# Later heads' probabilities turned by VectorE in 32x32 blocks and placed by a DRAM write and four reads, in place of TensorE's transposes

## The chip, the cores and the metric

The kernel runs on one core of a Trainium2 chip. The metric is the device time of one execution in microseconds (us). The kernel before takes 1205.58 us, the median of three runs that lie between 1205.02 and 1205.92 us. The engines are named as in the profile: PE is TensorE, DVE is VectorE, ACT is ScalarE, POOL is GpSimd, and SP is SyncE, which here only issues DMAs.

## What is computed

Eight batches of eight attention heads with a decay, 576 tokens and a head width of 64, and behind them a feed-forward block with a layer norm.

```python
scores = q @ k.T / 8 + (cum[:, None] - cum[None, :])     # causal, per head
attn   = softmax(scores)
x      = concat_heads(attn @ v)                          # (8, 576, 512)
xn     = (x - mean(x)) / sqrt(var(x) + 1e-6) * g_ln
out    = x + relu(xn @ w_ch1) @ w_ch2                    # w_ch1: 512 x 2048, w_ch2: 2048 x 512
```

To multiply the probabilities with `v` on PE, the key index has to lie on the partitions, while the softmax has the query index there. The 576 x 576 probabilities of a head must therefore be turned.

## The kernel before

The order of the work is written out by hand. The 64 heads are cut into four row units each, `t` = 1 to 4 (unit 1 takes the first 64 rows, `t` = 0, along); unit `t` has 128 query rows and 192, 320, 448 or 576 keys. One loop runs over the 256 units, and each turn of it is a **slot**. A slot emits the pieces that a string of letters in `ORDERS` names, in that order; all engines run their own instructions in the order in which they were emitted, so the string sets what stands ahead of what on each engine. In the third string, which holds from slot 66 on: `Q` scores of this unit (PE), `S` mask and row minimum (DVE), `A` product with `v` of an older unit (PE), `e` exponential (ACT), `t` and `h` and `l` the turning of an older unit (PE, ACT, DVE), `B` the division by the row sum (DVE makes the reciprocal, POOL multiplies), `M` the first feed-forward product of one step (PE, 12 matmuls of 256 columns), `N` the second one of the step before (PE, 6 matmuls of 512 columns), `r` and `m` the ReLU and its low part (ACT, DVE), `P` and `D` preparations and loads.

The feed-forward work is 18 chunks of 256 tokens by 16 steps, 288 steps in all. From slot 35 on a slot carries one step, and the steps that are left when the slots are used up follow alone. So PE has, in each slot, one step and the attention matmuls of the unit, in one line.

The first 16 heads ("full") compute in f32. The later 48 split each operand in a high part of the type fp32r and a low part, the rest, and add up two or three cheaper products. Only these 48 are touched in substance. For them a unit goes this way before: `softmax_b` scales the rows `p` on POOL (L428) and copies them by a DMA into a tile `pw` of the type fp32r (L441); two slots after its scores (`LAG` = 2) `transpose_unit` turns 128 x 128 pieces of `pw` on PE into a PSUM bank `tr` (L447, by `tr`); `transposed_hi` rounds them on ACT into the high part `ph` (L505); `transposed_lo` makes the low part `pl`, or the lower half of `ph`, on DVE (L510). Three slots after the scores of unit 2 and of unit 4 `av_unit` multiplies (L544): first the products with the high part (`o<-ph,vv`), then those with the low part (`o<-pl,vv`).

```python
def softmax_b(h, t):                       # L428: POOL
    nc.gpsimd.tensor_scalar(out=pt[:m, :w], in0=pt[:m, :w], scalar1=st[:m, 3:4], ...)
def transposed_lo(h):                      # L510: DVE
    nc.vector.tensor_tensor(out=lo, in0=tp, in1=hi.bitcast(F32), op=ALU.subtract)
```

Of the kernel before, what the change touches and what calls it, by code (L numbers as in the profile page):

```python
# [17 lines left out]
P = 128  # L18
# [10 lines left out]
LAG = 2  # L29
FIRST_MOE = 35  # L30
# [21 lines left out]
    (37, "WwQSstAMhPelgNFrfmBDLRba"),  # L52
    (66, "QSAFteahBlMPrmNbRLD"),
# [4 lines left out]
def attn_moe(ctx: ExitStack, tc: tile.TileContext, qk, v, f, g, w1, w2, out):  # L58
# [21 lines left out]
    ident0 = work.tile([P, P], F32, tag="p", bufs=3, name="ident0")  # L80
# [26 lines left out]
    fa = work.tile([B * H, S], F32, tag="p", bufs=3, name="fa")  # L107
    fb = work.tile([B * H, S], F32, tag="p", bufs=3, name="fb")
    fc = work.tile([B * H, S], F32, tag="p", bufs=3, name="fc")
    fones = work.tile([B * H, 704], F32, tag="ph1", bufs=1, name="fones")[:, 0:S]  # L110
# [197 lines left out]
    def load(n):  # L308
        h = Head()
        h.n, h.full = n, n < NFULL  # L310
        if h.full:
            h.kl = work.tile([66, S], F32, tag="kl", bufs=2, name=f"kl{n}")
            if len(xfs) < 2:
                xfs.append(new_xq(f"xf{n}", F32))
            h.xq = xfs[n % 2]
            nc.sync.dma_start(out=h.xq[0:64, :], in_=qk[n][0:64, 0, :])
            nc.sync.dma_start(out=h.kl[0:64, :], in_=qk[n][0:64, 1, :])
            if n > 0:
                nc.sync.dma_start(out=h.kl[64:66, :], in_=cumd[n])
# [15 lines left out]
    def prep_a(h):  # L335
# [47 lines left out]
    corners, padded, words = [], {}, []  # L383
# [39 lines left out]
    def softmax_b(h, t):  # L423
# [7 lines left out]
        if not h.full:  # L431
            if t == 0:
                if not words:
                    words.append(pools["late"].tile([P, D], F32R, tag="pw0", bufs=1, name="pw0"))
                    nc.gpsimd.memset(words[0].bitcast(F32), 0.0)
                pw = words[0]
            elif t % 2 == 0:
                pw = pools["late"].tile([P, S], F32R, tag="pw", bufs=1, name=f"pw{h.n}_{t}")
            else:
                pw = work.tile([P, S], F32R, tag="p", bufs=3, name=f"pw{h.n}_{t}")  # L440
            nc.sync.dma_start(out=pw[:m, :w].bitcast(F32), in_=pt[:m, :w])  # L441
            h.p[t] = (pw, st)
# [12 lines left out]
    def transpose_unit(h, t):  # L455
# [3 lines left out]
        if t <= 2:  # L459
            if t == 1:  # L460
                if h.full:
                    h.ph1 = padded_keys("ph1", 704, S1)
                else:
                    h.ph1 = work.tile([P, 704], F32R, tag="ph1", bufs=1, name=f"ph1_{n}")
                h.pl1 = None if h.full else pools["late"].tile([P, 384], F32R, tag="pl1", bufs=1, name=f"pl1_{n}")
            ph = h.ph1
            pl = ph if h.full else h.pl1
            tp = bank(f"tr{n}_{t}")
            if t == 1:
# [3 lines left out]
                work_.append((tp[0:64, 0:192], ph[0:64, 0:192], ph[64:128, 0:192]))  # L473
                work_.append((tp[:, 192:320], ph[:, 320:448], pl[:, 0:128]))
            else:
# [3 lines left out]
                work_.append((tp[0:64, 0:128], ph[0:64, 192:320], ph[64:128, 192:320]))  # L479
                work_.append((tp[:, 128:384], ph[:, 448:704], pl[:, 128:384]))  # L480
        else:
            if t == 3:
                if h.full:
                    h.ph2 = padded_keys("ph2", 9 * P, S - S1)
                else:
                    h.ph2 = work.tile([P, 9 * P], F32R, tag="ph2", bufs=1, name=f"ph2_{n}")
                h.pl2 = None if h.full else pools["late"].tile([P, 7 * P], F32R, tag="pl2", bufs=1, name=f"pl2_{n}")
            c = 0 if t == 3 else P
            ph = h.ph2[:, : 8 * P].rearrange("p (k c) -> p k c", k=4)[:, :, c : c + P]
            pl = None if h.full else h.pl2[:, : 6 * P].rearrange("p (k c) -> p k c", k=3)[:, :, c : c + P]  # L490
# [3 lines left out]
            work_.append((tp[0:64, 0, :], ph[0:64, 0, :], ph[64:128, 0, :]))  # L494
            work_.append((tp[:, 1:4, :], ph[:, 1:4, :], pl))
            if t == 4:
                tb = bank(f"tr{n}_4b")[:, :P]
                tr(tb, pt[:, 64 + 3 * P : 64 + 4 * P])
                work_.append((tb, h.ph2[:, 8 * P :], None if h.full else h.pl2[:, 6 * P :]))
# [3 lines left out]
    def transposed_hi(h, t):  # L503
        for tp, hi, lo in h.parts:
            nc.scalar.copy(out=hi, in_=tp)  # L505

    def transposed_lo(h):
        if not h.full:
            for tp, hi, lo in h.parts:
                nc.vector.tensor_tensor(out=lo, in0=tp, in1=hi.bitcast(F32), op=ALU.subtract)  # L510

    def av_unit(h, t):
# [25 lines left out]
        vv = h.vv  # L538

        def both(k):  # L540
            return vv[:, k].rearrange("p a d -> p (a d)")

        def acc(o, st, mv, first=False):
            mm(o, st, mv, start=first, stop=True, skip_group_check=True)  # L544

        if t == 2:
            ph, pl, w, c0 = h.ph1, h.pl1, S1, 0
# [3 lines left out]
            acc(po[0:64, 192:320], vv[:, 2, 0, :], pl[:, 256:384])  # L551
            acc(po[0:64, 64:320], vv[:, 1, 0, :], pl[:, 0:256])
        else:
            ph, pl, w, c0 = h.ph2, h.pl2, S - S1, S1
            for k in range(4):
                acc(po[:, 0:256], both(k), ph[:, 256 * k : 256 * k + 256], k == 0)
            acc(po[:, 128:256], both(4), ph[:, 8 * P :])
            acc(po[0:64, 128:256], vv[:, 4, 0, :], pl[:, 6 * P :])
            for k in range(1, 4):
                acc(po[0:64, 0:256], vv[:, k, 0, :], pl[:, 256 * (k - 1) : 256 * k])  # L560
        h.o = (po, w, c0)
# [233 lines left out]
    slots += [None] * (LAG + 1)  # L795
# [15 lines left out]
    for u, slot in enumerate(slots):  # L811
# [8 lines left out]
        if before(LAG + 1) is not None and before(LAG + 1)[1] in (2, 4):  # L820
            av = hd[before(LAG + 1)[0]]
# [7 lines left out]
        def piece(c):  # L829
            tu = before(LAG)  # L830
            if c == "t" and tu is not None:
# [3 lines left out]
            elif c == "l" and tu is not None:  # L835
                transposed_lo(hd[tu[0]])
# [3 lines left out]
            elif c == "A" and av is not None:  # L840
                av_unit(av, before(LAG + 1)[1])
# [18 lines left out]
            elif c == "R":  # L860
                moe.limit = min(NCHUNK, max(0, u - LAG - 1) // (4 * H) * S // C)
# [23 lines left out]
        def next_raw():  # L885
# [14 lines left out]
            elif n == NFULL - 1 and t == 1:  # L900
                load_raw(hd[NFULL], 0)
            elif t in (2, 3) and NFULL < n + 2 < B * H:
                if t == 2:
                    start_head(n + 2)
                load_raw(hd[n + 2], 1 if t == 2 else 0)

        def prep():

            if slot is not None:
                if t == 1 and n + 1 < NFULL:  # L910
                    start_head(n + 1)
                if n + 1 >= NFULL and n + 1 < B * H:
                    if t == 2:
                        prep_a(hd[n + 1])
                    if t == 3:
                        prep_b(hd[n + 1])
                if not h.full and t == LAG + 1:
                    prep_v(h)
                if t == LAG + 1 and h.full and n + 1 < B * H:
                    load_v(hd[n + 1])  # L920
                if t == LAG + 2 and not h.full and n + 1 < B * H:
# [52 lines left out]
```

## Time and profile before

| | |
|---|---|
| median of three runs | 1205.58 us |
| the profiled execution: its time | 1204.13 us |
| the profiled execution: its span, first to last instruction | 1202.3 us |
| DVE busy | 751.5 us (63%) |
| ACT busy | 621.1 us (52%) |
| POOL busy | 457.3 us (38%) |
| moved by DMA | 139.00 MB |

A row of a group gives the line of the kernel, the engine and the operation, what it writes and reads, the shape, the count, and behind the bar the busy time in us and the mean of one in ns. A row of the timeline gives the start in us from the span's start, the duration in us, the engine, line and operation, the shape and how many instructions the row merges; in brackets the idle time of the engine before it and what ended it. A row of the windows gives, for a stretch, the busy time of each engine, then the granted clock of PE as a share of full speed, the mean busy share of the DMA engines and their GB/s. Matmuls overlap: the time from the start of one to the start of the next tells what one occupies, and its duration is longer.

### The profile page before, as it was taken

What the parts mean: (1) busy time and instruction counts of PE and PEld (TensorE: products, weight loads), DVE (VectorE), ACT (ScalarE), POOL (GpSimd) and SP (SyncE); (2) the same over time, 40 slices, a digit from 0 to 9 for tenths busy, and PEclk for the clock granted to TensorE, in tenths of its full rate; (3) what the DMA queues carried; (4) which work ended last, traced back from release to release, by engine and by line L of the source; (5) the groups of instructions that cost most, each with busy time, mean ns of one, the idle gap of its engine ahead of it and who ended that gap; (6) DMA issues with size and microseconds to landing.
All of it is one profiled execution on the core that took longest, in us unless ns stands there. A gap on an engine that the chain in (4) does not pass through costs nothing.

```text
span 1202.3 us, 25770 instructions
## 1 busy us (share of the span) xinstructions
PE 1182.2 (98%) x8368; PEld 1064.2 (89%) x8368; DVE 751.5 (63%) x2658; ACT 621.1 (52%) x1936; POOL 457.3 (38%) x774
## 2 busy tenths in 40 slices
PE   8889999999999999999999999999999999999998
PEld 6567888999999999999999999999999999999997
DVE  6787684576767767777777777767676753122222
ACT  5887575555555555555555555655565532111111
POOL 3445345344545444443545454444454510000000
PEclk9999999999999999999999999999999999999999
DMA  6455442344444343434443434444344321111100
GB/s 194 142 157 170 132 134 84 96 139 132 134 134 134 128 140 125 139 129 145 133 146 123 139 127 132 138 125 143 125 138 132 116 88 40 31 36 40 32 28 26
DMA packets 127541, 139.00 MB, mean 116 GB/s; under 512 B 32432, under 2 KB 100016, under 8 KB 127408
## 3 DMA queue, kind: packets, MB, share of 16 engines
q1 hardware_dynamic: 127408, 137.36, 37.3%
q8 instruction: 67, 1.10, 0.4%
q14 instruction: 66, 0.54, 0.1%
HBM read 79.61 MB, written 19.17 MB: 82 GB/s over the span
## 4 chain that ended last, share of the span: by engine, by line
PE 89%; DVE 4%; ACT 2%; DMA 2%; issue 1%; POOL 0%; SPq 0%; DVEq 0%; ACTq 0%; POOLq 0%
PE h L624 12%; PE h L626 11%; PE h L625 11%; PE acc L646 11%; PE acc L647 11%; PE acc L648 11%; PE o L544 6%; PE tr L447 4%; PE s L378 3%; PE s L377 3%; PE s L375 2%; PE o L519 2%; PE tr L449 1%; DVE p L410 1%; ACT p L421 1%; DMA pw<-p 1%
## 5 line engine op out<-in xcount | busy, mean ns | idle before, releaser
L428 POOL TENSOR_SCALAR p<-p,st 64x64 f32<-64x64 f32 (+4 forms) x320 | 169.6, 535 | 493.3 <-ACT ph L505 173.7
L624 PE MATMUL h<-x,w1h 128*128 128x256 f32 x1152 | 339.2, 294 | 0.4 <-DVE st L410 0.4
L626 PE MATMUL h<-x,w1l 128*128 128x256 f32 x1152 | 325.6, 283 | 0.0
L625 PE MATMUL h<-x,w1h 128*128 128x256 f32 x1152 | 325.4, 282 | 0.0
L421 ACT ACTIVATE p<-p,st 64x64 f32<-64x64 f32 (+4 forms) x320 | 179.1, 560 | 210.2 <-DVE st L410 206.2
L637 DVE SCALAR_TENSOR_TENSOR hh<-h,hh 128x256 fp32r<-128x256 f32 x288 | 120.4, 418 | 186.7 <-ACT hh L632 184.2
L646 PE MATMUL acc<-w2h,hh 128*128 128x512 f32 x576 | 228.1, 396 | 0.0
L647 PE MATMUL acc<-w2l,hh 128*128 128x512 f32 x576 | 227.5, 395 | 0.0
L648 PE MATMUL acc<-w2h,hh 128*128 128x512 f32 x576 | 225.5, 391 | 0.0
L624 PEld LDWEIGHTS h<-x,w1h 128*128 128x128 f32 x1152 | 218.9, 190 | 5.4 <-issue 0.9
L625 PEld LDWEIGHTS h<-x,w1h 128*128 128x128 f32 x1152 | 219.7, 191 | 2.5
L626 PEld LDWEIGHTS h<-x,w1l 128*128 128x128 f32 x1152 | 219.5, 190 | 0.0
L632 ACT ACTIVATE hh<-h 128x256 fp32r<-128x256 f32 x288 | 110.0, 382 | 180.7 <-PE h L626 180.0
L410 DVE CUSTOM_DVE_ANT_0 p<-s,mask 64x64 f32<-64x64 f32 (+4 forms) x320 | 131.0, 423 | 22.5 <-PE s L378 15.0
L648 PEld LDWEIGHTS acc<-w2h,hh 128*128 128x128 f32 x576 | 108.3, 188 | 24.8
L426 DVE TENSOR_SCALAR st<-st 128x1 f32<-128x1 f32 (+1 forms) x320 | 48.1, 150 | 120.7 <-ACT p L421 117.8
L646 PEld LDWEIGHTS acc<-w2h,hh 128*128 128x128 f32 x576 | 109.3, 190 | 14.1 <-ACT ph_full L505 0.2
L647 PEld LDWEIGHTS acc<-w2l,hh 128*128 128x128 f32 x576 | 109.3, 190 | 11.8
L505 ACT CAST ph<-tr 64x128 fp32r<-64x128 f32 (+4 forms) x384 | 107.4, 328 | 3.7 <-PE tr L447 1.4
L580 ACT COPY ot<-o 64x320 f32<-64x320 f32 x96 | 38.0, 396 | 117.4 <-PE o L544 115.4
L510 DVE TENSOR_TENSOR pl<-tr,ph 128x128 fp32r<-128x128 f32 x192 | 88.0, 458 | 4.4
L377 PE MATMUL s<-hi 128*128 128x288 f32 (+4 forms) x288 | 81.8, 297 | 0.0
(90 smaller groups left out, 1884.1 us busy)
## 6 DMA issues: line engine op xcount, KB each, us to landing
raw<-in_qk_dram SPq DMA_DIRECT2D x96, 288.0 KB
wr<-in_w_dram SPq DMA_DIRECT2D x32, 512.0 KB
pw<-p SPq DMA_DIRECT2D x48, 288.0 KB
pw<-p SPq DMA_DIRECT2D x48, 224.0 KB
vr<-in_v_dram SPq DMA_DIRECT2D x64, 160.0 KB
out_dram<-xt SPq DMA_DIRECT2D x36, 256.0 KB
pw<-p SPq DMA_DIRECT2D x48, 160.0 KB
xa<-xs SPq DMA_DIRECT2D x32, 160.0 KB
```

Source lines behind the costliest of these rows:

```text
L377: mm(sp, h.hi[:, 0, q0 : q0 + m], h.hi[:, 1, a:z], start=True, stop=False)
L410: nc.vector.tensor_tensor_reduce(out=pt[:m, a:z], in0=sp, in1=mask[:m, off + a : off + z], scale=-SCALE, scalar=3.0e38 if i == 0 else st[: ...
L421: nc.scalar.activation(pt[:m, :w], pt[:m, :w], AF.Exp, bias=st[:m, i : i + 1], scale=-1.0, accum_out=st[:m, 2:3])
L428: nc.gpsimd.tensor_scalar(out=pt[:m, :w], in0=pt[:m, :w], scalar1=st[:m, 3:4], scalar2=1.0, op0=ALU.mult, op1=ALU.mult)
L624: mm(ph, w1h[:, k, fs], c.x[k][:, 0, :], start=(k == 0), stop=False)
L625: mm(ph, w1h[:, k, fs], c.x[k][:, 1, :], start=False, stop=False)
L626: mm(ph, w1l[:, k, fs], c.x[k][:, 0, :], start=False, stop=(k == KT - 1))
L632: nc.scalar.activation(h[:, 0, :], c.ph, AF.Relu)
L637: nc.vector.scalar_tensor_tensor(out=h[:, 1, :], in0=ph, scalar=0.0, in1=h[:, 0, :].bitcast(F32), op0=ALU.max, op1=ALU.subtract)
L646: mm(c.acc[i], h[:, 0, ts_], w2h[:, j, :], start=(j == 0), stop=False)
L647: mm(c.acc[i], h[:, 0, ts_], w2l[:, j, :], start=False, stop=False)
L648: mm(c.acc[i], h[:, 1, ts_], w2h[:, j, :], start=False, stop=(j == FT - 1))
```

## The change

For the 48 later heads PE no longer turns the probabilities. One slot after its scores (`T`) a unit is turned by DVE, in blocks of 32 x 32, into one tile `pb`; after units 2 and 4 SP writes `pb` to DRAM (`pd`, 128 x 768 or 128 x 1152 elements). Two slots after the scores (`V`, `READ`) four DMAs read it back, one for each 32 partitions, so that each block arrives on its partitions (`pt1`, `pt2`). Four slots after (`HIGH`) ACT makes the high part (`H` and `G`), DVE the low part of the first 64 keys (`l`), and POOL the low part of all others (`o`), in place in `pt`: one instruction of 128 x 896 elements for units 3 and 4, one of 128 x 384 for units 1 and 2. The product follows five slots after (`DONE`) instead of three, and reads `ph` for its high and `pt` for its low products. The columns are now in blocks of 32 with strides, and unit 2's first product takes 384 columns instead of 320. The split of the keys, queries and values moves to other slots (`k`, `x`, `P`), and the copy of the queries from DVE to ACT.

```diff
+READ, HIGH, DONE = 2, 4, 5
...
-    (37, "WwQSstAMhPelgNFrfmBDLRba"),
-    (66, "QSAFteahBlMPrmNbRLD"),
+    (37, "WwkQSTstAMhPeHlgNFGrxfmBoVDLRba"),
+    (66, "kQSTAHeVGFtlahBoMPrxmNbRLD"),
...
-            nc.sync.dma_start(out=pw[:m, :w].bitcast(F32), in_=pt[:m, :w])
-            h.p[t] = (pw, st)
...
+    def turn(h, t):
...
+        nc.vector.transpose(out_[rows, 0:2, first, :], pt[:m, 0:64].rearrange("p (b i) -> p b i", i=32))
+        if t > 0:
+            nc.vector.transpose(
+                out_[:, :, rest : rest + t, :].rearrange("p b k i -> p k b i"),
+                pt[:, 64 : 64 + P * t].rearrange("p (k b i) -> p k b i", b=4, i=32),
+            )
...
+    def write(h, t):
+        w = (6 if t == 2 else 9) * 32
+        pd = dram.tile([P, 4 * w], F32, tag=f"pd{t}", bufs=2, name=f"pd{t}_{h.n}")
+        nc.sync.dma_start(out=pd, in_=turned[0][:, : 4 * w])
...
+    def read(h, t):
...
+        for b in range(4):
+            r = z if b > 1 else 0
+            nc.sync.dma_start(
+                out=pt[32 * b : 32 * b + 32, :].bitcast(F32).rearrange("j (a r) -> j a r", a=4)[:, :, r:],
+                in_=src[b][:, :, r:],
+            )
...
+    def high_first(h, t):
...
+        nc.scalar.copy(out=ph[0:64, :, 0:z, :], in_=pt[0:64, :, 0:z, :].bitcast(F32))
+    def high_rest(h, t):
+        z, pt, ph = parts_of(h, t)
+        nc.scalar.copy(out=ph[:, :, z:, :], in_=pt[:, :, z:, :].bitcast(F32))
+    def low_first(h, t):
+        z, pt, ph = parts_of(h, t)
+        nc.vector.tensor_tensor(
+            out=ph[64:128, :, 0:z, :], in0=pt[0:64, :, 0:z, :].bitcast(F32), in1=ph[0:64, :, 0:z, :].bitcast(F32),
+            op=ALU.subtract,
+        )
+    def low_rest(h, t):
+        z, pt, ph = parts_of(h, t)
+        nc.gpsimd.tensor_tensor(
+            out=pt[:, :, z:, :], in0=pt[:, :, z:, :].bitcast(F32), in1=ph[:, :, z:, :].bitcast(F32), op=ALU.subtract
+        )
...
-            acc(po[:, 0:320], both(0), ph[:, 0:320], True)
-            acc(po[:, 64:320], both(1), ph[:, 320:576])
-            acc(po[:, 192:320], both(2), ph[:, 576:704])
+            acc(0, 384, 0, 0, True)
+            acc(128, 384, 1, 3)
+            acc(256, 384, 2, 5)
```

The names in the rows that follow carry the head and the unit: `p46_4` are the rows of head 46, unit 4, `pt2_45` is what head 45's units 3 and 4 became, `o45_4` their product with `v`.

On POOL, before, these instructions stand between unit 3 and unit 4 of head 46 and behind them:

```order
L428 TENSOR_SCALAR p46_3_10479<-p46_3_10479,st46_3_10480 128x448
L351 TENSOR_TENSOR hi47_10449<-raw47_0_10284,hi47_10449 64x576
L358 TENSOR_TENSOR vv46_10528<-vr46_10323,vv46_10528 128x5x64
L714 TENSOR_TENSOR rs8_10337<-rs8_10337 128x2
L715 TENSOR_TENSOR rs8_10337<-rs8_10337,sv8_10336 128x2
L716 TENSOR_SCALAR rs8_10337<-rs8_10337 128x2
L717 TENSOR_TENSOR rs8_10337<-rs8_10337 128x2
L714 TENSOR_TENSOR rs8_10337<-rs8_10337 128x2
L715 TENSOR_TENSOR rs8_10337<-rs8_10337,sv8_10336 128x2
L428 TENSOR_SCALAR p46_4_10554<-p46_4_10554,st46_4_10555 128x576
```

And now, from unit 4 of head 46 to the place two slots on:

```order
L443 TENSOR_SCALAR p46_4_9980<-p46_4_9980,st46_4_9981 128x576
L513 TENSOR_TENSOR pt2_45_9871<-pt2_45_9871,ph2_45_9986 128x4x224
L783 TENSOR_SCALAR rs8_9781<-rs8_9781 128x2
L784 TENSOR_TENSOR rs8_9781<-rs8_9781 128x2
L345 TENSOR_TENSOR kl48_10031<-raw48_1_9970,hi48_10030 64x576
L443 TENSOR_SCALAR p47_1_10041<-p47_1_10041,st47_1_10042 128x192
L443 TENSOR_SCALAR p0_1_177<-p0_1_177,st47_0_10044 64x64
L365 TENSOR_TENSOR vv46_10085<-vr46_9972,vv46_10085 128x5x64
L443 TENSOR_SCALAR p47_2_10106<-p47_2_10106,st47_2_10107 128x320
L513 TENSOR_TENSOR pt1_46_9989<-pt1_46_9989,ph1_46_10112 128x4x96
L356 TENSOR_TENSOR hi48_10030<-raw48_0_10100,hi48_10030 64x576
```

The two subtractions of L513 are new, and each stands right behind the scaling of another unit's rows in the same slot: the one of head 45's unit 4 behind `p46_4`.

On PE, the next slot opens with the scores of head 47's unit 1, and directly behind them stands the product of head 45's units 3 and 4:

```order
L385 MATMUL s47_0_0_10038<-kl47_9786,xq1_2840 64x128
L606 MATMUL o45_4_10050<-ph2_45_9986,vv45_9840 128x256 x4
L606 MATMUL o45_4_10050<-ph2_45_9986,vv45_9840 128x128
L606 MATMUL o45_4_10050<-pt2_45_9871,vv45_9840 64x256 x3
L606 MATMUL o45_4_10050<-pt2_45_9871,vv45_9840 64x128
```

Before, this place of the slot of unit 1 held the product of units 1 and 2 of the head before and four transposes of its unit 3:

```order
L378 MATMUL s47_0_0_10607<-kl47_10450,xq1_2933 64x128
L544 MATMUL o46_2_10615<-ph1_46_10494,vv46_10528 128x320
L544 MATMUL o46_2_10615<-ph1_46_10494,vv46_10528 128x256
L544 MATMUL o46_2_10615<-ph1_46_10494,vv46_10528 128x128
L544 MATMUL o46_2_10615<-pl1_46_10495,vv46_10528 64x128
L544 MATMUL o46_2_10615<-pl1_46_10495,vv46_10528 64x256
L447 MATMUL tr46_3_10626<-identr_71,pw46_3_10508 128x128 x3
L447 MATMUL tr46_3_10626<-identr_71,pw46_3_10508 64x128
```

The four transposes are gone, and the products with `pt2_45` read what L513 wrote in the slot before.

More of the change, by code (lines that the diff above doesn't have):

```diff
@@ L398, in corner, with row_tile @@
         return corners[n % 2]
+    def row_tile(h, t):
+        nm = f"p{h.n}_{t}"
+        if h.full and (4 * h.n + t - 1) % 3 == 0:
+            if "late" in pools:
+                return pools["late"].tile([P, 4 * 9 * 32], F32, tag="pb", bufs=1, name=nm)[:, 0:S]
+            return wpool.tile([P, S], F32, tag="p", bufs=1, name=nm)
+        return work.tile([P, S], F32, tag="p", bufs=2, name=nm)
     def softmax_a(h, t):
@@ L430, in softmax_b @@
         )
[L431 to L440, printed above, removed]
-            nc.sync.dma_start(out=pw[:m, :w].bitcast(F32), in_=pt[:m, :w])
-            h.p[t] = (pw, st)
+    SLOTS = {0: (0, 0), 1: (1, 3), 2: (2, 4), 3: (0, 2), 4: (1, 5)}
@@ new lines, in blocks @@
+    def blocks(tile_, t):
+        w = 6 if t <= 2 else 9
+        return tile_[:, : 4 * w * 32].rearrange("p (b r i) -> p b r i", b=4, i=32)
+    def turn(h, t):
+        if not turned:
+            turned.append(pools["late"].tile([P, 4 * 9 * 32], F32, tag="pb", bufs=1, name="pb"))
+            nc.gpsimd.memset(turned[0], 0.0)
+        pt, out_ = h.p[t][0], blocks(turned[0], t)
+        first, rest = SLOTS[t]
+        m = QT[t][1]
+        rows = slice(64, P) if t == 0 else slice(0, P)
+        nc.vector.transpose(out_[rows, 0:2, first, :], pt[:m, 0:64].rearrange("p (b i) -> p b i", i=32))
[4 more added lines that the diff above has]
+            )
@@ L460, in transpose_unit @@
             if t == 1:
[L461 to L465, printed above, removed]
+                h.ph1 = padded_keys("ph1", 768, S1)
             ph = h.ph1
-            pl = ph if h.full else h.pl1
             tp = bank(f"tr{n}_{t}")
@@ L503, in transposed_hi @@
     def transposed_hi(h, t):
-        for tp, hi, lo in h.parts:
+        for tp, hi in h.parts:
             nc.scalar.copy(out=hi, in_=tp)
[L507 to L510, printed above, removed]
     def av_unit(h, t):
@@ L819, in attn_moe @@
         av = None
-        if before(LAG + 1) is not None and before(LAG + 1)[1] in (2, 4):
-            av = hd[before(LAG + 1)[0]]
+        for back in (LAG + 1, DONE):
+            if before(back) is not None and before(back)[1] in (2, 4) and hd[before(back)[0]].full == (back == LAG + 1):
+                av, av_t = hd[before(back)[0]], before(back)[1]
         want = moe.can(wp.ready()) and u >= FIRST_MOE
@@ L830, in piece @@
             tu = before(LAG)
+            if tu is not None and not hd[tu[0]].full:
+                tu = None
+            late = before(HIGH)
+            if late is not None and (hd[late[0]].full or late[1] in (1, 3)):
+                late = None
+            due_read = before(READ)
+            if due_read is not None and (hd[due_read[0]].full or due_read[1] in (1, 3)):
+                due_read = None
+            past = before(1)
+            if past is not None and hd[past[0]].full:
+                past = None
             if c == "t" and tu is not None:
@@ L834, in piece @@
                 transposed_hi(hd[tu[0]], tu[1])
-            elif c == "l" and tu is not None:
-                transposed_lo(hd[tu[0]])
+            elif c == "T" and past is not None:
+                for i in [1, 0] if past[1] == 1 else [past[1]]:
+                    turn(hd[past[0]], i)
+                if past[1] in (2, 4):
+                    write(hd[past[0]], past[1])
+            elif c == "V" and due_read is not None:
+                read(hd[due_read[0]], due_read[1])
+            elif c == "H" and late is not None:
+                high_first(hd[late[0]], late[1])
+            elif c == "G" and late is not None:
+                high_rest(hd[late[0]], late[1])
+            elif c == "l" and late is not None:
+                low_first(hd[late[0]], late[1])
+            elif c == "k":
+                two = before(2)
+                if two is not None and two[1] == 4 and not hd[two[0]].full:
+                    values_low(hd[two[0]])
+                if slot is not None and n + 1 >= NFULL and n + 1 < B * H and t in (1, 3):
+                    (keys_high if t == 1 else queries_high)(hd[n + 1])
+                    (keys_low if t == 1 else queries_low)(hd[n + 1])
+            elif c == "x" and slot is not None and n + 1 >= NFULL and n + 1 < B * H and t == 3:
+                queries_copy(hd[n + 1])
+            elif c == "o" and late is not None:
+                low_rest(hd[late[0]], late[1])
             elif c == "Q" and slot is not None:
@@ L911, in prep @@
                     start_head(n + 1)
[L912 to L921, printed above, removed]
+                if t == LAG + 1 and h.full:
                     load_v(hd[n + 1])
```

132 lines of the change are left out of this document (77 added, 55 removed).

## The prediction

> **What bounds the kernel now.** I read the page first, then two stretches of the windows, one with attention and one with feed-forward alone, then one head of the timeline engine by engine.
>
> ```profile
> span 1202.3 us, 25770 instructions
> PE 1182.2 (98%) x8368; PEld 1064.2 (89%) x8368; DVE 751.5 (63%) x2658; ACT 621.1 (52%) x1936; POOL 457.3 (38%) x774
> PE 89%; DVE 4%; ACT 2%; DMA 2%; issue 1%; POOL 0%; SPq 0%; DVEq 0%; ACTq 0%; POOLq 0%
> ...
> 600.00:700.00 100.00, 100.00 (x732) 92.94 (x731) 71.90 (x260) 56.62 (x180) 44.34 (x66) 1.00 0.43 133
> 1000.00:1100.00 100.00, 100.00 (x648) 90.73 (x647) 25.48 (x59) 18.70 (x49) 5.50 (x28) 1.00 0.11 32
> ```
>
> PE bounds it: the chain that ended last is 89% PE, and in both stretches PE never pauses, at the full clock (1.00). From 600 to 700 us DVE (72%), ACT (57%), POOL (44%) and the DMA engines (0.43) have room. The feed-forward steps that do not fit into the slots run alone at the end. So whatever PE is spared among the later heads arrives at the end in full, and so does every wait that PE gets there.
>
> **What goes from PE.** Each pair of rows is the start of a unit's transposes and of what follows them on PE.
>
> ```profile
> 599.80 0.38 PE L447 MATMUL tr<-identr,pw 128*128 128x128 f32 x3
> ...
> 600.16 0.34 PE L624 MATMUL h<-x,w1h 128*128 128x256 f32 x1
> ...
> 604.42 0.34 PE L447 MATMUL tr<-identr,pw 128*128 128x128 f32 x3
> 604.60 0.33 PE L624 MATMUL h<-x,w1h 128*128 128x256 f32 x1
> ...
> 608.01 0.35 PE L447 MATMUL tr<-identr,pw 128*128 128x128 f32 x3
> 608.21 0.34 PE L624 MATMUL h<-x,w1h 128*128 128x256 f32 x1
> ...
> 611.97 0.43 PE L447 MATMUL tr<-identr,pw 128*128 128x128 f32 x4
> 612.25 0.35 PE L624 MATMUL h<-x,w1h 128*128 128x256 f32 x1
> ```
>
> The four slots of a head give 0.36 + 0.18 + 0.20 + 0.28 = 1.02 us, and 48 heads 49.0 us. The 64 more columns of unit 2's first product cost back about 0.03 us a head (the five products of 1152 columns below take 0.54 us), 1.4 us in all. Reading columns in blocks of 32 I take as free; no row shows such an operand, and I let half of the 0.9 us a head of products, up to 20 us in all, count as the far end. **PE is spared 47.6 us.**
>
> **What PE will wait for.** The new step is the subtraction on POOL (L513). The order puts it behind the scaling of another unit in the same slot, and PE wants its result in the next slot, right behind the scores there. First unit 4: how long PE takes from the scores of a unit 4 to the product that stands behind the next scores.
>
> ```profile
> 607.88 0.30 PE L378 MATMUL s<-kl,xq 66*128 66x288 f32 x1
> ...
> 611.43 0.53 PE L544 MATMUL o<-ph,vv 128*128 128x320 f32 x3
> 611.79 0.34 PE L544 MATMUL o<-pl,vv 128*64 128x128 f32 x2
> ...
> 603.46 0.70 PE L544 MATMUL o<-ph,vv 128*128 128x256 f32 x5
> 604.00 0.58 PE L544 MATMUL o<-pl,vv 128*64 128x128 f32 x4
> ```
>
> The product starts 611.43 - 607.88 = 3.55 us after the last scores began, 3.35 without the 0.20 of transposes between. It is now the product of units 3 and 4, whose high part takes 604.00 - 603.46 = 0.54. So PE reaches the low products, which read L513's result, after **3.89 us**. Now the other engines from the same scores on:
>
> ```profile
> 609.06 0.08 DVE L410 DVE_READ_ACCUMULATOR2_ANT st<- 128x1 f32 x1
> 609.18 0.78 ACT L421 ACTIVATE p<-p,st 128x576 f32<-128x576 f32 x1 [2.00 <-DVE st L410]
> 610.08 0.15 DVE L426 TENSOR_SCALAR st<-st 128x1 f32<-128x1 f32 x1 [0.94 <-ACT p L421]
> 610.70 0.75 POOL L428 TENSOR_SCALAR p<-p,st 128x576 f32<-128x576 f32 x1 [1.06 <-ACT ph L505]
> ...
> L410 DVE CUSTOM_DVE_ANT_0 p<-s,mask 64x64 f32<-64x64 f32 x64 | 13.4, 210 | 0.0
> L510 DVE TENSOR_TENSOR pl<-tr,ph 128x384 fp32r<-128x384 f32 x96 | 53.6, 558 | 2.2
> L591 DVE TENSOR_TENSOR xs<-o,ot 64x256 f32<-64x256 f32 x48 | 20.0, 416 | 17.4 <-ACT ot L580 17.2
> L230 POOL TENSOR_TENSOR w1l<-wy,w1h 128x512 fp32r<-128x512 f32 x16 | 20.5, 1281 | 0.0
> L609 POOL TENSOR_TENSOR x<-xr,x 128x256 fp32r<-128x256 f32 x6 | 4.3, 731 | 0.4 <-ACT x L607 0.4
> ```
>
> DVE has read the minimum at 609.14 and then waits 0.94 us for the exponential. Into that gap now fall the turning of unit 3 (64 and 384 columns) and the low part of 64 x 256. No row shows a 32 x 32 turn; the nearest of 64 and of 384 columns take 0.21 and 0.56, the low part like L591 0.42, so DVE is free at 610.33 instead of 610.08: 0.25 us late. (The bounds: nothing, if the turns run at twice the rate, and 0.8 us, if at half.) POOL's scaling then starts 610.70 - 607.88 + 0.25 = 3.07 after the scores and ends at 3.82. POOL's two-input subtractions take 731 ns for 256 and 1281 for 512 columns, 2.15 ns a column; 896 columns then take 1.28 + 384 x 0.00215 = 2.10 us. It ends at 5.92, and with 0.1 for the handing over (between the 0.04 from 609.14 to 609.18 and nothing seen from POOL to PE) PE goes on at 6.02. **PE waits 6.02 - 3.89 = 2.1 us in each head.** ACT's part (0.4 and, by its casts, some 0.96 us) hides in the 2.00 us before the exponential and in the scaling behind it.
>
> Unit 2 in the same way:
>
> ```profile
> 599.65 0.31 PE L378 MATMUL s<-kl,xq 66*128 66x320 f32 x1
> 600.42 0.08 DVE L410 DVE_READ_ACCUMULATOR2_ANT st<- 128x1 f32 x1
> 601.22 0.15 DVE L426 TENSOR_SCALAR st<-st 128x1 f32<-128x1 f32 x1 [0.72 <-ACT p L421]
> 601.83 0.54 POOL L428 TENSOR_SCALAR p<-p,st 128x320 f32<-128x320 f32 x1 [2.98 <-PE h L626]
> ```
>
> PE's product in the next slot starts at 603.46, less 0.36 of transposes 3.45 after the scores, and its high part takes 611.79 - 611.43 + 0.03 = 0.39: low products at 3.84. DVE reads the minimum at 600.50 and gets three turns (64, 128 and 64 columns, 0.7) and a low part of 64 x 384 (0.5), free at 601.70 instead of 601.22, 0.48 late. POOL scales from 2.66 to 3.20, subtracts 384 columns (0.731 + 128 x 0.00215 = 1.0) to 4.20, PE goes on at 4.30: 0.46 us. Together **2.56 us a head**; the last head has no softmax in front of its subtraction, so 47 heads wait: 120 us. PE is in one line, so the feed-forward step behind the product waits too.
>
> **The clock.** A wait of 2 us may cost more than itself:
>
> ```profile
> 89.20:92.60 3.40, 2.35 (x13) 1.00 0.28 82
> 92.60:96.10 3.50, 3.50 (x21) 0.51 0.35 124
> 65.30:68.70 3.40, 2.50 (x18) 1.00 0.69 227
> ```
>
> After 3.4 us in which PE was busy for 2.35 the clock was halved for the next 3.4 us; after 2.50 of 3.40 at 65.3 it was not. If these stretches run on by themselves, a gap of 2.1 us often leaves one of them with over 1.05 us idle. The limit is known from one event; I let half of the 47 waits cost 1.7 us (half of 3.4), 40 us, less 9 us of unit 2's waits that a slower PE covers: 31 us. The ends are 0 and 80 us. The Trainium skill, "TensorE: Matmul & The Clock Gate", The HAM clock gate, has the clock fall after at least one idle window of about 3.4 us. By that rule a gap of 2.1 us costs nothing more (the second rival); the trace has one fall after a window that was not idle.
>
> **What costs nothing.** DVE loses L510 and the queries' copy and gains turns and low parts of similar length, so its 72% stays. DMA: a head's copies of 0.78 MB become 0.98 MB written and 0.82 MB read. At 133 / 0.43 = 309 GB/s the longest write takes 1.9 us, and `pb` is wanted again a slot (over 3.3 us) later; the reads have two slots. If that cover is gone, DVE waits in its line at the next turn, ahead of the reciprocals, and each us there is one more us of unit 2's wait, 47 us in all.
>
> **The sum.** 1204.1 (the profiled execution's time) - 47.6 + 120 + 31 = 1308 us; the median of the runs is 1.5 us above that execution, so 1309 us.
>
> **The rivals.**
> 1. *The wait without the clock*: 1204.1 - 47.6 + 120 + 1.5 = 1278 us. For it: one event only, and the rule above. Against it: that event.
> 2. *Not slower*: POOL subtracts at the price of its one-input rows.
>
> ```profile
> L428 POOL TENSOR_SCALAR p<-p,st 128x576 f32<-128x576 f32 x64 | 48.3, 754 | 76.6 <-ACT ph L505 31.0 <-DVE st L427 12.4 <-ACT w1h L226 9.2
> L428 POOL TENSOR_SCALAR p<-p,st 128x192 f32<-128x192 f32 x64 | 27.3, 427 | 102.6 <-ACT p L421 93.0 <-DVE st L426 8.8 <-POOL p L428 0.3
> ```
>
> At 0.85 ns a column 896 take 1.03 us; with DVE's delay hidden, unit 4's wait is 3.57 + 1.03 + 0.1 - 3.89 = 0.8 us and unit 2's nothing: 38 us against 47.6, 1196 us. It decides at a wait of 1.0 us a head (47.6 / 47). Both two-input rows speak against it. With no wait at all it would be 1158 us.
> 3. *Transfers pile up*: the write holds `pb` over a slot; with 1 us a head more and the clock, 1370 us and above. The free DMA share speaks against it.
>
> **How the numbers follow.** Waits with clock losses, the forecast, 0.52; rival 1, 0.32; rival 2 with its neighbours 0.10; rival 3, 0.06. About 0.2% is what a measurement of this kernel can tell from no change. Faster 0.08, same 0.02, slower 0.90. The range: below, waits of 1.9 us a head without clock loss (DVE's delay hidden, POOL as forecast for unit 4, unit 2 nearly free) give 1247; above, 3 us a head and 60 us of clock give 1360; I take 1247 to 1365, which leaves out rivals 2 and 3.
>
> **What would show it.** PE should sit idle before L606's low products, released by POOL's L513, about 2.1 us in the slots of unit 1 and 0.5 in those of unit 3, 47 times each; L513 should take 2.1 and 1.0 us; the clock's digits should fall below 9 among the later heads (rival 1: not). If L513 takes about 1 us, or PE's waits name DVE or a DMA, the working is wrong at that place; if the waits are as forecast and the time is not, the clock or the price of the strided columns is.

## The result, and the profile after

The changed kernel takes 1284.72 us (median of four runs, 1282.83 to 1288.27) against 1205.75 us (four runs) before: the ratio is 1.0658, with an interval of 1.0634 to 1.0683. The profiled execution took 1285.22 us, its span 1283.2. The time lies inside the range, between the forecast (1309) and the first rival (1278).

The page of the changed kernel, the line of the busy time:

```profile
PE 1159.3 (90%) x7648; PEld 1025.9 (80%) x7648; DVE 770.7 (60%) x2706; ACT 646.2 (50%) x1744; POOL 594.3 (46%) x870
```

A stretch of its windows (busy us of PE, PEld, DVE, ACT, POOL, then the granted clock, the DMA share, GB/s):

```profile
600.00:700.00 100.00, 86.53 (x574) 78.18 (x573) 69.57 (x247) 54.53 (x144) 60.85 (x87) 1.00 0.59 178
```

PE, which never paused from 600 to 700 us before, now has 13.5 us of 100 without work, at the full clock. Nothing else is full: DVE has 70%, POOL 61%, the DMA engines 0.59. An engine that bounds a kernel and still stands idle waits in its line, so the waits of the changed kernel come next (engine, line waited for, us in total, times, longest):

```profile
PEld o L606 <- POOL pt L513: 115.4, 94, 2.7
PE o L606 <- POOL pt L513: 97.8, 64, 2.5
...
DVE pb L461 <- DMA pd<-pb: 3.5, 3, 2.2
```

And the groups of the new instructions:

```profile
L513 POOL TENSOR_TENSOR pt<-pt,ph 128x896 fp32r<-128x896 f32 x48 | 100.5, 2093 | 5.5 <-ACT ph L502 5.5
L513 POOL TENSOR_TENSOR pt<-pt,ph 128x384 fp32r<-128x384 f32 x48 | 49.1, 1022 | 0.5 <-ACT ph L502 0.5
L463 DVE STREAM_TRANSPOSE pb<-p 128x384 f32<-128x384 f32 x48 | 25.7, 535 | 0.0
L506 DVE TENSOR_TENSOR ph<-pt,ph 64x256 fp32r<-64x256 f32 x48 | 20.1, 419 | 1.5
```

The low products wait for POOL's subtraction 94 times, twice in each of 47 heads, 115.4 us by the loads of their weights (PEld; PE's own row is shorter, since the tail of the high products covers a part of each wait). By unit, the products of units 3 and 4 hold 86.9 us of it, 1.85 in each head. Those of units 1 and 2 hold 28.5: 0.25 to 0.58 us in 35 heads and 1.3 to 1.8 in the other 12. The subtraction takes 2093 and 1022 ns, a turn of 384 columns 535. The write of `pb` holds DVE back three times.

The list also puts 57.6 us of POOL's idle time ahead of the scaling down to the reads (`POOL p L443 <- DMA pt<-pd`); but in all 22 of these waits the scaling starts 0.17 us behind the end of the reciprocal (L442) that it needs, as it does where the list names the reciprocal, so the reads don't hold it.

The timeline of POOL and PE at the end of unit 4's slot and the start of the next shows how a wait comes about:

```profile
613.85 0.29 PE L385 MATMUL s<-kl,xq 66*128 66x288 f32 x1
...
616.68 0.75 POOL L443 TENSOR_SCALAR p<-p,st 128x576 f32<-128x576 f32 x1 [0.91 <-DVE st L442]
...
617.14 0.75 PE L606 MATMUL o<-ph,vv 128*128 128x256 f32 x5
...
617.40 2.08 POOL L513 TENSOR_TENSOR pt<-pt,ph 128x896 fp32r<-128x896 f32 x1
...
619.53 0.63 PE L606 MATMUL o<-pt,vv 128*64 128x256 f32 x4 [1.64 <-POOL pt L513]
```

POOL scales unit 4's rows first, because they stand ahead in its line, and only then makes the low part of the head before, which PE wants at 617.68 (617.14 and the 0.54 us of the high products). PE goes on at 619.53: 1.85 us late. The scaling starts 2.83 us after the last scores began, where it started 2.82 after them before (610.70 - 607.88 in the prediction's rows).

### The profile page after: what moved, and what is told of

Read it like the earlier page. It is cut to its first block, busy times and chain, and to the rows that moved or that the text cites. A ratio compares the mean times of both kernels' runs of the same rounds, so it can differ in the third digit from the quotient of the medians.

```text
span 1283.2 us, 24610 instructions
## 1 busy us (share of the span) xinstructions
PE 1159.3 (90%) x7648; PEld 1025.9 (80%) x7648; DVE 770.7 (60%) x2706; ACT 646.2 (50%) x1744; POOL 594.3 (46%) x870
## 5 line engine op out<-in xcount | busy, mean ns | idle before, releaser
L443 POOL TENSOR_SCALAR p<-p,st 64x64 f32<-64x64 f32 (+4 forms) x320 | 169.6, 535 | 434.6 <-DVE st L442 196.7
L691 PEld LDWEIGHTS h<-x,w1h 128*128 128x128 f32 x1152 | 221.6, 192 | 5.5 <-issue 0.9
L692 PEld LDWEIGHTS h<-x,w1h 128*128 128x128 f32 x1152 | 222.9, 193 | 2.5
L693 PEld LDWEIGHTS h<-x,w1l 128*128 128x128 f32 x1152 | 223.1, 194 | 0.0
L513 POOL TENSOR_TENSOR pt<-pt,ph 128x384 fp32r<-128x384 f32 x96 | 149.5, 1558 | 6.1 <-ACT ph L502 6.1
L606 PE MATMUL o<-pt,vv 128*64 128x256 f32 (+1 forms) x288 | 48.9, 278 | 101.4 <-POOL pt L513 97.8
L715 PEld LDWEIGHTS acc<-w2h,hh 128*128 128x128 f32 x576 | 109.7, 190 | 25.3
L713 PEld LDWEIGHTS acc<-w2h,hh 128*128 128x128 f32 x576 | 111.3, 193 | 14.5 <-ACT ph_full L568 0.2
L606 PEld LDWEIGHTS o<-pt,vv 128*64 128x64 f32 x288 | 29.6, 135 | 115.4 <-POOL pt L513 115.4
L658 DVE TENSOR_TENSOR xs<-o,ot 64x320 f32<-64x320 f32 x96 | 43.2, 450 | 125.8 <-ACT ot L647 125.8
L776 POOL TENSOR_SCALAR sv<-sv 128x2 f32<-128x2 f32 x18 | 3.9, 215 | 188.9 <-DVE sv L760 187.7
```

Of the source, the lines that this page charges most:

```text
L513: nc.gpsimd.tensor_tensor(out=pt[:, :, z:, :], in0=pt[:, :, z:, :].bitcast(F32), in1=ph[:, :, z:, :].bitcast(F32), op=ALU.subtract)
L691: mm(ph, w1h[:, k, fs], c.x[k][:, 0, :], start=(k == 0), stop=False)
L692: mm(ph, w1h[:, k, fs], c.x[k][:, 1, :], start=False, stop=False)
L693: mm(ph, w1l[:, k, fs], c.x[k][:, 0, :], start=False, stop=(k == KT - 1))
L713: mm(c.acc[i], h[:, 0, ts_], w2h[:, j, :], start=(j == 0), stop=False)
L715: mm(c.acc[i], h[:, 1, ts_], w2h[:, j, :], start=False, stop=(j == FT - 1))
```

## The experiments

The theory (A) is that PE waits because L513 stands late in POOL's line. Its rivals are the clock (B), the transfers or the strided columns (C), and, once the first runs were in, two more (D, E) for what was left.

**The casts and the subtraction ahead of the exponential** (`e1_all_early`)

```diff
-    (66, "kQSTAHeVGFtlahBoMPrxmNbRLD"),
+    (66, "kQSTAHGoeVFtlahBMPrxmNbRLD"),
```

> ACT's two casts and POOL's subtraction L513 move ahead of the exponential and of the scaling in the same slot; nothing is left out. Theory A (PE waits because L513 starts only behind the exponential, the reciprocal and the scaling of another unit): L513 then starts about 1.4 us after the scores and ends at 3.5, before PE wants it at 3.9; the 117 us of waits go, and with them the halved clock: 1204.1 - 47.6 = 1157 us, up to 1170 if the scaling, now behind L513, makes the next slot's turns late; ratio to before 0.96 to 0.97. Theory B (the clock is what costs, set off by something else): the low digits stay, over 1190 us. Theory C (transfers or the strided columns cost the time): it stays within 20 us of 1285.

Measured: 1201.28 us (1200.44 to 1203.69), ratio 0.996 (0.9945 to 0.9975). 83 us of the 128 us that lie between 1284.7 and 1157 are gone, with nothing left out and no transfer changed, so C falls. The number that B had (over 1190) is met, but not by the clock, which is at 1.00 over the later heads:

```profile
240.00:950.00 710.00, 674.03 (x4504) 614.11 (x4505) 557.60 (x1917) 434.79 (x1105) 458.44 (x604) 1.00 0.66 198
```

44 us remain, more than A had. Two rows of its waits say where (the third, ACT's wait for a load, matters further down), and one group what has changed:

```profile
PEld o L606 <- DVE ph L506: 28.4, 23, 2.1
...
PEld o L606 <- POOL pt L513: 13.5, 15, 1.3
...
ACT hi L350 <- DMA raw<-in_qk_dram: 51.8, 29, 3.5
```

```profile
L506 DVE TENSOR_TENSOR ph<-pt,ph 64x256 fp32r<-64x256 f32 x48 | 54.6, 1138 | 1.7 <-ACT ph L498 0.2
```

PE's wait for POOL fell from 115.4 to 13.5 us, and a new one of 28.4 us came up behind DVE's small low part L506, whose 256 columns now take 1138 ns instead of 419. 1157 + 28.4 + 13.5 is 1199.

**Only the subtraction ahead of the scaling** (`e2_sub_ahead`)

```diff
+    (66, "kQSTAHeVGoFtlahBMPrxmNbRLD"),
```

> Only L513 moves ahead of the scaling L443; ACT's casts stay behind the exponential. Theory A: unit 4's exponential ends at about 616.15 in the slot looked at, the cast of 0.93 us then ends at 617.1, and L513 starts there instead of at 617.4: 0.3 us a head, 14 us; unit 2's cast is 0.5 us and its scaling 0.54, so L513 starts up to 0.5 us earlier and most of its 29 us go: 1245 to 1265 us. Theory A' (the place behind the scaling alone is the cause, as in the forecast's words): L513 starts 0.75 and 0.54 us earlier, all of unit 2's waits go and 35 us of unit 4's: 1220. Theory C: 1285.

Measured: 1254.77 us, ratio 1.0393 (1.0368 to 1.0417). Its waits:

```profile
POOL pt L513 <- ACT ph L502: 159.0, 74, 7.5
PEld o L606 <- POOL pt L513: 75.8, 59, 1.6
```

PE's wait for L513 fell by 40 us, of which the time shows 30; the low and high products now also wait 6.6 us for DVE's L506 and 3.1 for the cast L502. POOL now waits for the cast (74 times), as A had it: L513 starts behind the cast and not as early as its new place alone would allow.

**Only the casts ahead of the exponential** (`e3_casts_early`)

```diff
+    (66, "kQSTAHGeVFtlahBoMPrxmNbRLD"),
```

> Only ACT's casts move ahead of the exponential; L513 stays behind the scaling. Theory A (POOL's line, not ACT's, sets L513's start): L513 starts as before, right behind the scaling, 1281 to 1290 us, and later by as much as the casts delay the exponential. A rival by which the wait for the cast ph is what counts: L513 earlier by 0.3 to 0.9 us, 1240 to 1270 us.

Measured: 1282.93 us (1275.86 to 1285.97), ratio 1.0625 (1.0589 to 1.066): no change that can be told from the changed kernel. Its wait:

```profile
PEld o L606 <- POOL pt L513: 112.3, 94, 2.6
```

An earlier input brings nothing while the instruction itself stands behind the scaling. For the whole gain both have to move, as in e1.

**The subtraction twice** (`e4_twice`)

```diff
+        for _ in range(2 if t == 4 else 1):
-        nc.gpsimd.tensor_tensor(
+            nc.gpsimd.tensor_tensor(
...
```

> L513 of units 3 and 4 runs twice (the same subtraction again, so the low products get other values): one more step of 2.09 us in 48 heads. Theory A: PE waits 2.09 us more in 47 heads, 98 us, so at least 1383. Then the clock: if a stretch of 3.4 us with PE busy for less than about 0.4 of it halves the next (what after's seven cases look like), waits of 3.9 us leave such a stretch in nearly every head: up to 47 x 1.7 = 80 us more, 1430 to 1465, with the granted clock at 0.6 to 0.8 in these stretches. If only a wholly idle stretch of 3.4 us halves it (the Trainium skill, TensorE: Matmul & The Clock Gate, The HAM clock gate), a wait of 3.9 us seldom holds one: 1383 to 1395. If L513 were hidden: 1285.

Measured: 1444.28 us (1441.85 to 1446.32), 159.6 us over the changed kernel. Its wait (the edit moves the lines by one):

```profile
PEld o L607 <- POOL pt L514: 210.8, 95, 4.7
```

The mean granted clock of this kernel, of the changed one, and of the one before:

```profile
core 0: 1441.4 us, clock 0.935
```

```profile
core 0: 1283.2 us, clock 0.987
```

```profile
core 0: 1202.3 us, clock 0.998
```

The wait grew by 95.4 us, 47 times 2.03, so the step is paid in full. The other 64 us are the clock. A mean of 0.987 over 1283.2 us is 33 us at half speed, 0.935 over 1441.4 us is 187 us; the 154 us more are 45 stretches of 3.4 us, about one in each of the 47 heads, and cost 64 us, where half speed for PE alone would be 77. What sets one off is read from the windows, a stretch and the next. Two such pairs of this kernel:

```profile
581.20:584.60 3.40, 0.00 (x0) 0.00 (x0) 2.92 (x9) 1.40 (x5) 3.32 (x2) 1.00 0.15 29
584.60:588.00 3.40, 3.02 (x14) 3.02 (x15) 1.22 (x6) 0.37 (x1) 2.37 (x4) 0.50 0.79 241
...
646.00:649.40 3.40, 1.22 (x10) 1.22 (x11) 0.10 (x1) 0.37 (x1) 3.34 (x2) 1.00 0.42 173
649.40:652.80 3.40, 3.40 (x14) 2.91 (x13) 2.01 (x8) 1.09 (x3) 1.65 (x4) 0.51 0.39 119
```

And four such pairs of the changed kernel:

```profile
564.60:568.00 3.40, 1.47 (x11) 1.32 (x12) 1.58 (x7) 1.73 (x7) 3.40 (x3) 1.00 0.40 141
568.00:571.40 3.40, 3.40 (x15) 3.11 (x14) 1.65 (x7) 1.04 (x3) 2.04 (x4) 0.51 0.66 223
...
878.60:882.00 3.40, 1.76 (x15) 1.54 (x14) 2.44 (x9) 2.50 (x8) 3.27 (x3) 1.00 0.40 103
882.00:885.40 3.40, 3.40 (x17) 3.30 (x16) 1.29 (x7) 0.86 (x3) 2.44 (x4) 0.51 0.76 260
738.70:742.10 3.40, 1.76 (x16) 1.61 (x15) 2.35 (x10) 2.13 (x7) 3.40 (x3) 1.00 0.12 41
742.10:745.50 3.40, 3.40 (x26) 3.09 (x25) 1.97 (x10) 0.78 (x2) 1.64 (x4) 1.00 0.84 271
...
615.80:619.20 3.40, 2.09 (x15) 1.72 (x13) 2.68 (x5) 2.50 (x7) 2.52 (x2) 1.00 0.42 121
619.20:622.60 3.40, 3.07 (x21) 2.90 (x22) 2.82 (x12) 2.03 (x7) 2.25 (x4) 1.00 0.15 62
```

A stretch with PE idle throughout is followed by a halved one, and so is one with PE busy for 1.22 or 1.47 us of 3.40; one of 2.09 is not, and at 1.76 it goes either way. Over all later heads, 24 of the 48 stretches at full clock ahead of a halved one in this kernel have PE busy for at most 0.10 us, the other 24 for 0.15 to 1.53; the eight of the changed kernel have 0.98 to 1.79; and in neither kernel did a stretch under 1.7 us go without a halved one behind it. A wait of 1.85 us leaves at most about that much idle in one stretch, so it seldom crosses the line; a wait of 4 us nearly always does.

The rule of the Trainium skill ("TensorE: Matmul & The Clock Gate", The HAM clock gate) has the clock fall after at least one idle window of about 3.4 us. Read as a wholly idle stretch, it covers about half of what is seen here, and none of the eight of the changed kernel; these decide against that reading. The time of 1444 us alone would not: the expectation of 1383 to 1395 us by this rule also took wholly idle stretches to be seldom, and they come in about half of the heads.

**Unit 4 early, unit 2 late** (`e8_unit4_early`): casts and L513 stand ahead of the exponential for units 3 and 4 alone.

```diff
-    (66, "kQSTAHeVGFtlahBoMPrxmNbRLD"),
+    (66, "kQSTAXeVYFtlahBoMPrxmNbRLD"),
...
+            elif c == "X" and late is not None:
+                high_first(hd[late[0]], late[1])
+                if late[1] == 4:
+                    high_rest(hd[late[0]], late[1])
+                    low_rest(hd[late[0]], late[1])
+            elif c == "Y" and late is not None and late[1] == 2:
+                high_rest(hd[late[0]], late[1])
...
-            elif c == "o" and late is not None:
+            elif c == "o" and late is not None and not (late[1] == 4 and u >= 66):
```

> The changed kernel with unit 4's casts and subtraction early, as in e1, and unit 2's left where they are. Theory A with the forecast's sizes (2.1 us a head for unit 4, 0.46 for unit 2): of the 84 us that e1 gained, unit 4 holds at least four fifths; unit 4's waits go down to what e1 leaves of them, about 48 us less, and the halved stretches go, 11 us: 1215 to 1235 us. If unit 2's waits and the clock weighed as much as unit 4's: above 1245.

Measured: 1223.68 us (1218.79 to 1228.3), ratio 1.0143 (1.011 to 1.0175). 61 of e1's 83 us, about three quarters, come from unit 4's place, a little under the four fifths that A had. Unit 4's waits for L513 fell from 86.9 to 3.7 us, but unit 2's, whose place did not change, rose from 28.5 to 47.2; why they rose wasn't followed up.

**The splits later** (`e5_splits_late`, `e6_low_ahead`, `e7_rstd_2`)

```diff
+    (66, "QSTAHGoeVFtlahBkMPrxmNbRLD"),     e5
+    (66, "QSHGolTAeVFtahBkMPrxmNbRLD"),     e6, and e7 with RSTD = 2 in place of 6
```

> e1_all_early, and the splits of the next head's keys and queries (letter k, ACT L350 and L342 first) move from the head of a slot to behind the scaling. e1 still stands 44 us above 1157. Theory D (in e1 ACT's cast L350 waits for the load raw<-in_qk_dram, 50.5 us in 28 waits, and holds back the exponential and the casts behind it, so that L513 of unit 4 starts late): about half of the 44 us go, 1175 to 1190 us. Theory E (what is left comes from DVE's low part L506 behind the turns, 28 us of PE's waits): 1197 to 1204 us.

> e5_splits_late, and DVE's low part L506 moves ahead of the turns in the same slot. Theory E: PE's 28 us of waits for L506 go and with them 15 to 28 us of the time, 1150 to 1185 us depending on e5. Theory D: nothing more than 5 us under e5, since L506's lateness is the load's.

> e6_low_ahead, and POOL's small operations on the norm's variance (L776 to L784, about 0.2 us each) come two in a slot instead of six. In e1 six of them stand ahead of L513 in some slots of a chunk and hold it back by up to 1.6 us. Theory A (whatever stands ahead of L513 on POOL is paid by PE): 5 to 12 us under e6. If POOL's line is no longer the limit: within 3 us of e6.

Measured: 1251.51, 1288.82 and 1333.34 us, all slower than e1: three misses. The waits name one oversight and one new effect, here of e5:

```profile
PEld o L606 <- POOL vv L365: 81.9, 47, 3.7
```

and here of e7:

```profile
PE acc L713 <- DVE xt L790: 47.7, 12, 4.3
```

In e6 the same wait takes 102.3 us, in e7 84.0. The letter `k` also issues the low part of the values (`values_low`, L365 on POOL), which the product of unit 2 reads in the next slot but one. Put behind the scaling it came late in all 47 heads. So these runs don't decide between D and E; they show once more what an instruction late in POOL's line costs. In e7 the norm's small operations, two in a slot, were not done when a chunk's output (L790) wanted them, and the next chunk's products waited.

**The values early again, the splits late** (`e9_values_early`, `e10_low_ahead`)

```diff
+    (66, "KQSTAHGoeVFtlahBkMPrxmNbRLD"),    e9: K is values_low alone, k the splits
+    (66, "KQSHGolTAeVFtahBkMPrxmNbRLD"),    e10: the low part l ahead of the turns T
```

> e5_splits_late again, but the low part of the values (POOL L365, which the letter k issued too) stays at the head of its slot, a letter of its own. In e5 unit 4's stalls fell from 50 to 20 us as theory D had it, and 58 to 74 us of new waits of PE name vv L365, which had come to stand behind the scaling in the slot ahead of the product that reads it. Theory A (PE pays for what stands late on POOL's line, whichever line it is): those waits go, e1's unit 4 falls by 30 us and its unit 2 stays at 10: 1165 to 1178 us. If e5's gain in unit 4 came from its slower slots alone: 1195 to 1203 us.

> e9_values_early, and DVE's low part L506 ahead of the turns in the same slot. In e5, L506 had all but gone from PE's waits (1.0 us). Theory D: within 4 us of e9, in either direction. Theory E: 10 us or more under e9.

Measured: e9 1239.2 us (1234.4 to 1240.66), e10 1219.54 us (1215.44 to 1228.96). e9 lies outside both of its ranges. ACT's wait L350 for the load has all but gone in e9 (1.1 us against 51.8 in e1), and yet it is 38 us slower than e1: PE's waits for L513 and L506 together grew from 41.9 to 69.7 us, and the mean granted clock fell from 0.994 to 0.982. This doesn't settle theory D, since the edit that takes ACT's wait away also puts POOL's split L356 ahead of L513. e10 is 20 us under e9, as E had it. One slot of e9 shows both engines at the place:

```profile
627.48 1.44 POOL L356 TENSOR_TENSOR hi<-raw,hi 64x576 fp32r<-64x576 f32 x1
629.00 2.10 POOL L513 TENSOR_TENSOR pt<-pt,ph 128x896 fp32r<-128x896 f32 x1
...
629.21 2.17 DVE L506 TENSOR_TENSOR ph<-pt,ph 64x256 fp32r<-64x256 f32 x1
...
631.43 0.81 PE L606 MATMUL o<-ph,vv 128*128 128x256 f32 x5 [0.62 <-DVE ph L506]
```

The split L356, now behind the scaling, puts L513 off to 629.00. DVE's L506 begins 0.21 us later and ends at 631.38, just behind L513's end at 631.10, where its 256 columns take 0.42 us by themselves. PE then waits for L506, not for L513. In e10 L506 stands ahead of the turns, and begins ahead of L513 in 45 of 48 heads, in e9 in 14: its mean falls from 1444 ns to 787.

**The norm's small operations behind the subtraction** (`e11_rstd_behind`): in some heads of e10 six of them, and the split, stand ahead of L513, as POOL's timeline shows there:

```profile
258.60 1.43 POOL L356 TENSOR_TENSOR hi<-raw,hi 64x576 fp32r<-64x576 f32 x1
260.11 0.26 POOL L781 TENSOR_TENSOR rs<-rs 128x2 f32<-128x2 f32 x1
...
261.54 0.45 POOL L782 TENSOR_TENSOR rs<-rs,sv 128x2 f32<-128x2 f32 x1
261.95 2.25 POOL L513 TENSOR_TENSOR pt<-pt,ph 128x896 fp32r<-128x896 f32 x1
```

The edit:

```diff
-            elif c == "L":
+            elif c == "L" and not (u >= 66 and slot is not None and t == 3):
```

> e10_low_ahead, and POOL's small operations on the norm's variance (L781 to L784) are left out of the slots of unit 3, where six of them, 0.28 us apart, stand ahead of unit 4's L513 in one head of each chunk; they come a slot later, behind it. In e10 most heads take 14.5 us and unit 1's slot 4.2 us, but in the 11 heads with these six it takes 6.7 to 7.8. Theory A: these 11 go down to 4.2 to 5 us, 25 us, and the halved stretches that follow them, 7 x 1.6 = 11: 1180 to 1195 us, below the kernel before. If the small operations only fill time in which L513 would wait for its cast anyway: 1210 to 1220 us.

Measured: 1209.28 us (12 runs), ratio 1.0022 (1.0008 to 1.0035). It gained 10 us, against the 25 to 40 expected. The first two rows are of e10, the other three of e11:

```profile
core 0: 1213.6 us, clock 0.987
...
PEld o L606 <- POOL pt L513: 48.9, 36, 3.1
...
core 0: 1208.2 us, clock 0.998
...
PEld o L606 <- POOL pt L513: 35.9, 46, 1.7
...
PE acc L713 <- DVE xt L790: 15.9, 11, 1.5
```

The wait for L513 fell by 13.0 us, and a new one of 15.9 took its place: in 11 chunks the operations, now behind L513, are late for the chunk's output, and PE waits there. So the 25 us that the expectation put on the waits did not come. What the run gained is mostly the clock, which the expectation had at 11 us: eight stretches of the later heads were halved in e10, none in e11.

**Three edits on e1** (`e12_all_three`)

```diff
+    (66, "kQSHGolTAeVDFtahBMPrxmNbRL"),
...
-            elif c == "L":
-                run_later(RSTD)
+            elif c == "L" and not (u >= 66 and slot is not None and t == 3):
+                run_later(8 if u >= 66 else RSTD)
```

> e1_all_early with three edits, one for each wait that it still shows: DVE's low part L506 ahead of the turns (28 us of PE's waits in e1, 5 in e10); the loads of the next head (letter D) issued ahead of the output copies on SP, so that raw<-in_qk_dram lands before ACT's L350 stands in line for it (50.5 us of ACT's waits in e1); and POOL's small operations left out of unit 3's slots, eight at a time instead of six. The splits stay at the head of the slot. Theory A (e1's last 44 us are what stands ahead of L506 and L513 in their lines): 1170 to 1190 us, ratio 0.97 to 0.985. If the transfers themselves are what is late (DMA share 0.66 to 0.69 in e1) and not their place in SP's line: 1190 to 1203 us, with ACT's wait for raw still above 35 us.

Measured: 1181.01 us (six runs, 1175.62 to 1186.57), ratio to before 0.979 (0.9767 to 0.9813). It beats both kernels and lies in A's range. The busy times of its page, and its waits:

```profile
PE 1139.5 (97%) x7648; PEld 1013.8 (86%) x7648; DVE 789.8 (67%) x2706; ACT 654.7 (56%) x1744; POOL 604.6 (51%) x870
...
PEld o L606 <- POOL pt L513: 21.5, 24, 1.3
...
ACT hi L350 <- DMA raw<-in_qk_dram: 10.6, 18, 1.2
...
PEld o L606 <- DVE ph L506: 2.5, 3, 1.1
```

Its stretch from 600 to 700 us:

```profile
600.00:700.00 100.00, 97.61 (x655) 88.64 (x654) 81.27 (x281) 63.31 (x162) 68.23 (x94) 1.00 0.68 202
```

PE now works 97.61 of 100 us there. ACT's wait for the load is down from 51.8 us in e1 to 10.6, while the DMA engines moved about as much (202 GB/s against 204 in e1 in the same stretch), so its place in SP's line was late and not the transfer. How the 20 us over e1 divide among the three edits wasn't measured; what the load alone cost e1 (theory D) stays open.

## Why the prediction came out as it did

- **What bounds.** Right: PE bounds, and what it is spared or made to wait arrives at the end in full. The accounts of the changed kernel, of e1 and of e4 close on that to within a few us.
- **47.6 us spared.** Right, by two readings of e12. Its 1181.0 us less its 24.0 us of waits is 1157.0; the sum without any wait was 1204.1 - 47.6 + 1.5 = 1158. And its page has PE busy for 42.7 us less than the 1182.2 before, with some 5 us more lost at half speed (mean clock 0.994 against 0.998), so some 47 us less work. The strided columns, which I took as free, leave no more than a few us.
- **120 us of waits.** Right in place and count: 94 waits, released by L513, which took 2.09 and 1.02 us for the 2.10 and 1.0 forecast. That the total of 115.4 us came out so near is in part luck, since two errors of opposite sign met in it. Unit 4's waits are 86.9 us, 1.85 a head for the 2.1 forecast: the 0.25 us by which DVE was to delay the scaling isn't there (the scaling starts 2.83 us after the scores in the slot above and 2.82 in the middle one of the 48 heads, against 3.07 forecast). Unit 2's are 28.5 us for the forecast 21.6: about 0.3 us in most heads, less than the 0.46 forecast, and about 1.5 in 12 heads, which the forecast didn't have. What makes these 12 differ stays open.
- **31 us of clock.** This is the term that was mis-sized. The step said that half of the 47 waits of unit 4 would halve the clock, from one early event (2.35 us busy of 3.40, then half speed). In the later heads a stretch of 2.09 of 3.40 had no such effect and the line lies near 1.76, so a wait of about 2 us mostly stays short of it: eight stretches were halved. The mean clock of 0.987 against 0.998 is 28.6 us more at half speed, in line with these eight, worth at most 14 us at 1.7 each. With it the account closes: 1204.1 - 47.6 + 115.4 + 14 = 1286 against 1285.2 measured. Why the early event fell at 2.35 stays open; the matmuls there are other ones (f32, of 66 to 128 rows).
- **Rival 1**, the wait without the clock, came closest (1278), since the clock cost less than half of what I gave it; but the rule that I named beside it (and once called the second rival's) is not the reason: eight stretches were halved behind stretches in which PE was busy for 0.98 to 1.79 us.
- **Rival 2** fell by the 2093 ns of L513: that is twice the 1.03 us that it took from the one-input scaling. **Rival 3** fell by DVE's 3.5 us of waits for the write, and by e1, which took 83 us off with every transfer in place.
- **What costs nothing** held while PE was waiting anyway. In e1, with PE faster, the same turns waited 19.6 us for the write of `pb`: the cover was partly the wait itself.

## What to carry to other kernels

When work is moved from the engine that bounds to one with room, ask first where it stands in that engine's line and which wait ends it: here POOL was 38% busy before, and a subtraction in the wrong place of its line, twice a head, cost more than twice what the bounding engine was spared. A new instruction that the bound engine reads soon belongs ahead of work that is read a slot later, together with its inputs, and its neighbours on the other engines have to be looked at again after it has moved. A gap that is short against the clock's stretch of 3.4 us cost little more than itself here; the next 2 us of it cost 1.7 times themselves (159.6 us for 95.4 us of wait).

## What the runs showed of the hardware that was not expected

DVE's subtraction of two SBUF operands stands still while POOL runs one. L506 of 256 columns takes 419 ns in the changed kernel, where it ends before L513 begins, 1138 ns on average in e1 and 1444 ns in e9, where they fall together. Two of e9's groups, L506 and the turn beside it:

```profile
L506 DVE TENSOR_TENSOR ph<-pt,ph 64x256 fp32r<-64x256 f32 x48 | 69.3, 1444 | 1.5
...
L463 DVE STREAM_TRANSPOSE pb<-p 128x384 f32<-128x384 f32 x48 | 25.7, 536 | 0.0
```

In e9 all 35 of these L506 that began while POOL was at L513 (34) or L356 (1) ended 0.28 us behind it, whenever they had begun, and took up to 2.36 us; one that began 0.04 us ahead of L513 took its usual 419 ns. The turn of 128 x 384, with one input, takes its usual time: the 35 in e1 that ran for at least a third of their time beside L513 or L356 took 536 ns on average, the other 13 took 535. The Trainium skill has this ("SBUF — State Buffer", SBUF: two separate sides): DVE with two SBUF inputs and GpSimd share a pair of ports under an exclusive lock, and the one that comes second is blocked for the whole instruction. The traces agree with it for a DVE instruction that comes second: 1444 ns on average in e9 against 419. The prediction didn't use it, since in the order of the change L506 runs before L513. It goes far to explain why the plain repair e1 stopped at 1201 us, where PE waits 28.4 us for L506; but a run that takes only this lock away, with L506 on another engine, wasn't tried.
